# A new order table for the same operations of a gated linear attention followed by a spatial gating unit

## Chip, cores and metric

The kernel runs on one core of a Trainium2 chip. The metric is the device time of one execution in microseconds (us), smaller is better. In the text PE is TensorE (its weight loads are shown apart, as PEld), DVE is VectorE, ACT is ScalarE, POOL is GpSimd and SP is SyncE, from whose queue the DMAs are issued.

## What is computed

Two layers. The first is linear attention with a decaying state, for 4 batches, 8 heads, 768 steps and a head size of 48; the second is a gated unit that mixes over the sequence:

```python
for t in range(S):                                   # S = 768, D = 48
    state = alpha[:, :, t, :, None] * state + einsum('bhd,bhe->bhde', k[:, :, t], v[:, :, t])
    y[:, :, t] = einsum('bhd,bhde->bhe', q[:, :, t], state)
x = y.transpose(0, 2, 1, 3).reshape(B, S, H * D)      # 4 x 768 x 384
h = maximum(x @ w_in, 0.0)                            # 384 -> 1024
u, v = h[..., :512], h[..., 512:]
v_n = (v - mean(v)) / sqrt(var(v) + 1e-06)            # over the last axis
v_s = einsum('ts,bsd->btd', w_spatial, v_n) + b_spatial[None, :, None]
out = (u * v_s) @ w_out                               # 512 -> 384
```

Inputs and output are float32; the kernel works in bfloat16 with float32 sums in PSUM.

## The kernel before

The 768 steps of a batch are cut into 6 chunks of 128, so there are 24 chunks, numbered 0 to 23 over the four batches 0 to 3. The recurrence is solved chunk by chunk with matmuls. Chunks 0 to 3 and 6 to 9 are taken four at a time, chunks 4 and 5 as a pair, the others singly.

The program does not issue instructions as it goes through its loops. It first makes a list of 944 operations (`op(key, engines, emit, deps, take, ...)`), each with the engines that may run it, the operations that it needs, and the PSUM banks that it takes. Then `replay` reads a table, `PLAN`, and issues the operations in the table's order, on the engine that the table names:

```python
for word in plan.split():
    word, *junk = word.split(":")
    word, *banks = word.split("@")
    op, eng = ops[int(word[1:])], LETTERS[word[0]]
    ...
    op.emit(eng)
```

A word `P103@6,4,5,7:512#7:424#7` means: operation 103 on PE, with banks 6, 4, 5 and 7, and before it two matmuls of 512 and 424 columns on a constant tile (`junk`) into bank 7, whose result nobody reads. Each engine runs its own words in the table's order and waits at the head of its queue when an input is not there; what stands behind a waiting instruction on that engine waits too. SP's words are the DMA issues.

The operations, by the names that this text uses (the number behind a name is the chunk or the pair of chunks, or batch and tile, or batch, column block and half):

- `ac`, `kc`, `qc`, `vc`: loads of alpha, k, q and v. With `.4` four chunks at a time, 768 KB each. `w_in`, `w_sp`, `w_out` are loads of weights, followed by casts to bfloat16 (`cast`). `w_sp` is also transposed on PE (`wt`) and evicted (`we`).
- `pr`: products of neighbouring alphas. `ln`: logarithm of alpha (ACT). `half`, `cum`, `cums`: running sums as matmuls. `einv`, `eexp`: exponentials of minus and plus these sums (ACT; `binv` is the tile of the first).
- `kt`, `qt`: k and q times these factors (`kt` on POOL or DVE, `qt` on DVE). `vb`, `vbs`: cast of v. `tr`, `trk`: transposes of `kt` and `qt` on PE, evicted by `ev`, `evs` into `kqT`. `causal`: the POOL selects that make a mask; `one` makes another.
- `upd`: the chunk's addition to the state (PE); `z`, `S`, `sb`: sum, decay and cast of the state. `sc`: scores (PE); `m`, `ms`: scores times mask (DVE, into `ptm`). `pm` spreads v over partitions, evicted by `vp`. `y`, `ya`: the chunk's output (PE); `xe` evicts it into `xT`.
- Second layer: `v`, `u`: the two halves of `x @ w_in`; `ve`, `ue`: their relu and eviction; `bn`: mean and variance of a tile (DVE); `rs`: the inverse root (ACT); `nm`: `shift`, minus mean times root (DVE); `vn`: normalisation, on ACT (line 1091, uses `shift`) or on DVE (line 1095, uses mean and root). `s`: the spatial matmul, first part over tiles 0 to 3, second part over tiles 4 and 5; `se`: adds the bias (DVE); `g`: times u (POOL or DVE); `o`: the matmul with `w_out`; `oe`: its eviction; `st`: the store. The last tile of the last batch is done in two halves of 192 columns, `o.3.5.0` and `o.3.5.1`.

The matmuls `v`, `u`, `s` and `o` use the whole array of 128 x 128; `tr`, `trk`, `wt`, `sc`, `y`, `ya` and `pm` use parts of it. `vn` reads

```python
if e == "ACT":
    nc.scalar.activation(out=vn[n2][:, x, :], in_=v_sb[n2][:, x, :], func=AF.Identity,
                         bias=shift[n2][:, x:x + 1], scale=rstd[n2][:, x:x + 1])
    return
nc.vector.tensor_scalar(out=vn[n2][:, x, :], in0=v_sb[n2][:, x, :], scalar1=mvs[n2][:, x, 0:1],
                        scalar2=rstd[n2][:, x:x + 1], op0=ALU.subtract, op1=ALU.mult)
```

and `nm` is issued for every tile, whichever engine normalises it. After the last operation of the table ten memsets of one column run on POOL.

Of the kernel before, what the change touches and what calls it, by code (L numbers as in the profile page):

```python
# [51 lines left out]
S278 S399 S389 D39 A206 S29 S387 A165 D166 D208 D168 A286 A294 D35 S388 S400 S401 S390 P210@1 P40@4,6 A288 A211 D42
D41 D212 D209 G297 G300 G306 P217@3 P290@1 P219@6 P221@4 A149 A150 A167 A220 D222 A213 D214 D298 P229@2 P237@6 P225@4
A295 D215 D307 A216 A289 D301 A291 A218 P233@5 A292 A296 P238 D239 P230 D231 P226 P43@3,0 P223@6 A44 A45 G27 G28 D304
D227 P234 D235 G303 A224 P46@1,3 P49@0,2 A47 A51 G236 G228 G299 G240 G232 D50 D48 P309@4,7 D310 P312@5,6 P315@0,1
P318@2,3 D316 D313 D311 D314 P249@4 P250 D251 A302 A317 A319 P341@2,7 P335@6,5 D343 A308 A320 A305 P245@1 P246
P321@7,3,4,0 D336 D337 S506 S548 D322 D324 P253@6 P333@7,5 P254 P241@3 P242 S494 D247 D255 A403 A391 A334 A340 P392@6
A323 P348@5,1 A393 D342 A394 S402 P344@2 P338@7 A345 G33 G32 G30 G325 G326 G31 S495 S507 D243 G396 D327 G328 D349 S560
S497 S496 D397 D350 S508 S509 P404@3 A405 A406 G407 P260@4 P257@5 S611 S549 S563 S550 S562 S561 A339 A395 A261 D408
D330 P362@2 P346@3,6 G398 G244 A363 D347 A353 A258 P354@7,1 P410@0,4 D356 D355 A411 P359@3 P413@1 G329 G331 D412  # L60
P351@5 P357@7 G256 G332 A510 G248 G409 P416@4,0 D414 G415 A352 P421@6,2 D418 D364 D417 A358 P369@1 D422 D423 A552 A498
A370 P374@0 A360 A375 P380@7 P499@1 A500 A502 P376@4 P511@0 A514 D361 D371 P419@6 P424@2 A420 A425 A512 A501 A513 A381
P263@3 P426@2 A365 D377 P372@6 A373 D427 D382 P438@4 P436@2 A437 A439 A264 D428 D516 G252 D366 P378@7 P429@6 A430
P440@4 D441 D431 A564 A383 A379 P442@3 A443 G503 G515 G505 P521@6 P272@0 G517 P529@4 P269@2 P266@3 S623 A432 D522
P565@6 D504 D368 P518@1,7 D433 P553@5 D384 D385 D386 S551 D530 D267 A270 A367 A434 A435 P452@2 S613 S614 S612 S624
P453 D454 A554 A555 D558 P444@3 P445 D446 D519 P456@2 P457 D458 D273 G455 S730 S625 G571 A520 A566 A567 A556 G557 S718
G569 A615 G531 A532 D570 P448@3 P449 P468@2 P469 D450 G459 A559 D470 P533@0,5 P524@3,1 G447 S626 S772 S719 G523
P572@7,4 D525 D534 D535 A574 S733 S721 P472@2 P473 P460@0 P461 P575@4 D526 D474 P616@5 A573 A568 A627 D576 D462 S732
S784 S731 S774 S786 S720 P527@1 P536@2 S775 S773 S835 S847 A617 A537 A618 A528 P579@4,6 P588@7,3 D580 G451 G622 G577
G620 S785 P464@0 D581 D621 D590 P584@4 P628@2 D585 D589 P465 A629 A630 A619 D632 D466 A734 G578 P541@6 P538@1 A542  # L70
P482@5 A539 A483 A722 G463 G631 G586 P476@4 G475 G471 G467 P735@2 P634@1,6 D543 P582@5 P591@0 D635 P637@1 P723@7 A636
A583 D477 D638 P640@4,6 D642 D592 A726 A736 A724 A738 A725 P645@5,3 P593@1 D646 D641 D647 G633 G587 P488@6 A489 D540
G639 P604@0 A776 A594 A737 A605 P596@5 P485@4 P777@1 D595 P643@3 P648@6 A544 P479@0 A644 G729 D545 A778 P491@3 A486
P598@4 G741 A547 A597 G727 D606 D480 A649 A607 P602@0 P650@5 P653@6 A492 A780 D740 D546 D599 P745@3 D651 D608 A609
A779 A603 A654 D746 D610 P660@4 D652 A788 D782 D655 P664@5 D728 D783 P662@3 A665 A663 P668@2 P672@0 P600@6 A601 A656
D657 A658 D661 D659 P789@5 A790 A791 G739 P753@3 D754 G781 G755 P680@1 P666@7 P676@6 A839 A747 A667 P673 P677 P681
P669 D674 D678 A851 A792 G679 G793 D682 P799@0 G683 D800 D670 P742@3,4 P692@1 P693 P696@2 D744 P840@4 A743 A841 D794
D694 P757@5,3 P796@0,7 D759 P748@1,6 D758 P697 D801 D749 D750 P688@3 S836 S837 S848 S849 A842 A798 A797 A843 D845
P852@5 A853 A854 D698 S268 S487 S787 S850 S274 S838 G675 G671 P684@7 D856 G844 P685 P706@0 P689 D690 G695 G855 P751@4
P760@2 D686 D761 A707 A752 P803@5,0 P858@6,1 D804 P812@3,4 A859 A860 A756 G802 G691 P703@7 G795 D814 D805 A704 P765@2  # L80
P762@6 A766 P808@1 D809 G699 G687 P700@0 A846 A701 P869@7,4 P864@1,5 D813 S705 S490 S702 G857 P806@2 P815@3 A807 A763
A816 G810 A811 P715@0 D767 D865 D866 P861@1 P820@6 P817@5 P709@3 P824@2 D862 D871 D870 G863 P872@7 A818 D764 P867@5
D873 P828@4 A868 D819 A829 D830 P822@5 A823 A768 A831 D769 D821 P712@7 P874@4 A875 D713 P877@5 P886@6 A887 D832 P884@4
D878 D770 P890@7 P826@6 P888@5 A771 D885 A833 D834 A825 A889 D876 D879 A880 P912@4 P896@2 P900@5 S484 P904@1 D827 D716
P892@0 S478 S708 S493 D881 D882 A883 P893 D894 P905 D906 G895 S717 P897 P901 P916@0 P913 P908@1 P917 P909 D898 G899
D907 D902 A710 S714 S265 A891 S481 S711 D903 P926@5 A927 P923@2 S271 S262 A924 D910 S259 P920@1 P921 G911 D914 D918
D915 S928 S925 P929@2 A930 S931 D919 D922 P941@0 D942 P938@1 A939 S943 S940 P935@5 P932@1 A933 D936 S937 S934
"""

PAIRS = (2,)
QUADS = (0,3)
PLAIN = (0, 2)

SPLIT = ()
SMALL = ()
# [33 lines left out]
def kernel(  # L131
# [295 lines left out]
    def pair(j):  # L427
# [22 lines left out]

        if j not in PLAIN:
            op(("pr", j, 1), "POOL DVE",
# [776 lines left out]
    idle = consts.tile([128, 1], FP32, name="idle")  # L1229
    nc.vector.memset(junk, 0.5)  # L1230
    replay(ops, held, warm, PLAN)
    for _ in range(10):
        nc.gpsimd.memset(idle, 0.0)


# [28 lines left out]
```

## Time and profile before

| | |
|---|---|
| median of 3 runs | 139.98 us (139.69 to 140.05) |
| the profiled execution | 139.9 us, of which 138.1 us from its first to its last instruction |
| granted TensorE clock | 0.998 |
| busy: PE, DVE, ACT, POOL | 129.9, 121.2, 108.8, 87.8 us |
| DMA | 28.66 MB, mean 207 GB/s |

A group row of the profile reads: line, engine, operation, output and inputs, shapes, count, then busy time and mean duration in ns, then the idle time before these instructions and what ended it. A timeline row reads: start in us, duration in us, engine, line, operation, output and inputs, count, and in brackets the idle time ahead of it and what ended that. A line can be that of a helper: 177 and 179 are copies, 183 and 185 relus, 188 products, 1004 the whole-array matmuls of the second layer.

### The profile page before, as it was taken

The page shows a single profiled execution, that of the slowest core. Times are in us where ns is not written, and L with a number is a line of the kernel's source. Part 1 is how long each engine was busy: PE and PEld are TensorE (multiplying, and loading weights), DVE is VectorE, ACT ScalarE, POOL GpSimd, SP SyncE. Part 2 cuts the span into 40 slices and gives each one's busy share as a digit, 9 for nine tenths or more (in the row PEclk, how much of TensorE's full clock was granted, in tenths as well). Part 3 has the DMA queues.
Part 4 walks back from the last instruction along what each step waited for, and adds up shares of the span by engine and source line. Part 5 has one row for each costly group of instructions (what it writes and reads, how often), then busy time and mean ns, then how long its engine had stood idle before and what let it go on. Part 6 is the DMA issues. An engine that isn't in the chain of part 4 may idle for free.

```text
span 138.1 us, 5300 instructions
## 1 busy us (share of the span) xinstructions
PE 129.9 (94%) x2110; PEld 79.6 (58%) x2124; DVE 121.2 (88%) x295; ACT 108.8 (79%) x258; POOL 87.8 (64%) x148
## 2 busy tenths in 40 slices
PE   6798999999999999999999999999999999999990
PEld 3255555665466556656667675655676665565550
DVE  6059999999899999999899999998999999897950
ACT  3483999999999599999959999969979793874221
POOL 7576799979369899950099999420499932002620
PEclk9999999999999999999999999999999999999999
DMA  3999999599989897798999899899910046007554
GB/s 90 372 370 381 347 343 360 136 376 388 339 186 278 162 211 140 141 210 176 206 209 210 169 203 202 168 207 264 209 29 5 0 169 241 0 0 268 190 196 148
DMA packets 76521, 28.66 MB, mean 207 GB/s; under 512 B 63056, under 2 KB 74960, under 8 KB 76496
## 3 DMA queue, kind: packets, MB, share of 16 engines
q1 hardware_dynamic: 76464, 28.32, 77.9%
q8 instruction: 16, 0.26, 0.8%
q14 instruction: 9, 0.07, 0.2%
q0 software_dynamic: 32, 0.00, 0.0%
HBM read 23.60 MB, written 4.72 MB: 205 GB/s over the span
## 4 chain that ended last, share of the span: by engine, by line
PE 56%; ACT 16%; DVE 13%; DMA 5%; issue 4%; POOL 3%; SPq 0%; POOLq 0%; ACTq 0%
PE bank L1004 37%; DMA vc<-in_v_dram 5%; ACT vn L1091 4%; DVE stats L1066 3%; PE bank L943 2%; ACT v_sb L183 2%; PE bank L959 2%; PE bank L415 2%; PE bank L987 2%; DVE uT L185 2%; ACT uT L183 1%; PE bank L835 1%; DVE ptm L842 1%; ACT kqT L177 1%; PE bank L853 1%
## 5 line engine op out<-in xcount | busy, mean ns | idle before, releaser
L188 POOL TENSOR_TENSOR gT<-vs,uT 128x384 bf16<-128x384 f32 x27 | 24.5, 922 | 21.7 <-DVE vs L1151 21.3
L1004 PE MATMUL bank<-w_spT,vn 128*128 128x384 bf16 x192 | 35.0, 327 | 0.5 <-ACT vn L1091 0.3
L1004 PEld LDWEIGHTS <-vn 128*128 128x128 bf16 x192 | 17.6, 98 | 13.2 <-ACT vn L1091 1.7
L188 POOL TENSOR_TENSOR kt<-kc,binv 128x384 bf16<-128x384 f32 x21 | 19.5, 935 | 3.4 <-ACT uT L183 2.2
L1004 PE MATMUL bank<-xT,w_in 128*128 128x384 bf16 x96 | 19.1, 326 | 0.1
L948 DVE TENSOR_TENSOR ptm<-bank,mask 128x512 bf16<-128x512 f32 x28 | 17.9, 681 | 0.5 <-PE bank L943 0.3
L1004 PE MATMUL bank<-w_out_sb,gT 128*128 128x384 bf16 (+1 forms) x100 | 18.3, 320 | 0.0
L1004 PE MATMUL bank<-w_in,xT 128*128 128x512 bf16 x58 | 17.3, 380 | 1.0 <-issue 0.3
L177 ACT COPY kqT<-bank 128x512 bf16<-128x512 bf16 (+1 forms) x20 | 15.5, 814 | 3.4 <-PE bank L770 2.4
L1151 DVE TENSOR_TENSOR vs<-bank,bsp_bc 128x384 f32<-128x384 f32 x31 | 16.2, 550 | 1.9 <-PE bank L1004 1.7
L1066 DVE BATCH_NORM_STATS2 stats<-v_sb 128x6 f32<-128x512 bf16 x24 | 16.4, 683 | 0.6 <-ACT v_sb L183 0.4
L1004 PEld LDWEIGHTS <-w_in 128*128 128x128 bf16 x96 | 8.9, 97 | 7.0 <-issue 1.0
L188 DVE TENSOR_TENSOR qt<-qc,bank 128x384 bf16<-128x384 f32 x24 | 12.8, 543 | 0.1
L183 ACT ACTIVATE v_sb<-bank 128x512 bf16<-128x512 f32 x20 | 11.9, 603 | 1.0 <-PE bank L1004 0.9
L1004 PEld LDWEIGHTS <-gT 128*128 128x128 bf16 x100 | 9.1, 98 | 5.8 <-POOL vb L179 0.2
L1091 ACT ACTIVATE vn<-v_sb,shift,rstd 128x512 bf16<-128x512 bf16 x13 | 10.0, 809 | 2.1 <-DVE shift L1083 2.0
L183 ACT ACTIVATE uT<-bank 128x384 bf16<-128x384 f32 x24 | 11.2, 492 | 0.4 <-DVE shift L1083 0.4
L177 ACT CAST xT<-bank 128x384 bf16<-128x384 f32 x21 | 9.9, 487 | 2.0 <-PE bank L415 1.6
L842 DVE TENSOR_TENSOR ptm<-bank,mask 128x512 bf16<-128x512 f32 x16 | 10.2, 682 | 0.2 <-PE bank L835 0.2
L1004 PEld LDWEIGHTS <-xT 128*128 128x128 bf16 x72 | 6.4, 98 | 6.2 <-issue 0.3
L392 DVE TENSOR_TENSOR zs<-bank,state 128x384 f32<-128x384 f32 x16 | 8.8, 552 | 0.6 <-ACT sbd L177 0.3
L241 PE MATMUL bank<-junk 128*128 128x512 f32 (+3 forms) x16 | 8.0, 629 | 1.1 <-DVE quarters_of L312 1.0
(159 smaller groups left out, 264.7 us busy)
## 6 DMA issues: line engine op xcount, KB each, us to landing
ac<-in_alpha_dram SPq DMA_DIRECT2D x14, 192.0 KB, 4.4
qc<-in_q_dram SPq DMA_DIRECT2D x14, 192.0 KB, 4.3
kc<-in_k_dram SPq DMA_DIRECT2D x14, 192.0 KB, 3.9
vc<-in_v_dram SPq DMA_DIRECT2D x14, 192.0 KB, 4.7
raw_w<-in_moe_w_spatial_dram SPq DMA_DIRECT2D x3, 768.0 KB, 6.7
out_dram<-raw_w SPq DMA_DIRECT2D x11, 192.0 KB, 2.1
out_dram<-o_sb SPq DMA_DIRECT2D x9, 192.0 KB, 2.0
ac<-in_alpha_dram SPq DMA_DIRECT2D x2, 768.0 KB, 6.7
```

Of the source, the lines that this page charges most:

```text
L177: nc.scalar.copy(out=out, in_=in_)
L183: nc.scalar.activation(out=out, in_=in_, func=AF.Relu)
L185: ENG[eng].tensor_scalar_max(out=out, in0=in_, scalar1=0.0)
L188: ENG[eng].tensor_tensor(out=out, in0=in0, in1=in1, op=ALU.mult)
L241: nc.tensor.matmul(out=banks[n][:, 0:cols].rearrange("p (a b) -> p a b", a=4), lhsT=junk, rhs=junk[:, None, 0:cols // 4].to_broadcast([128 ...
L392: lambda _: nc.vector.tensor_tensor(out=zs[i % 3], in0=tp(), in1=state[(i - 1) % 3], op=ALU.add),
L842: nc.vector.tensor_tensor(out=ptm[n2][:, ci, s], in0=banks[sl.bank].rearrange("p (hp t) -> p hp t", hp=HP), in1=mask[:, 3][:, None, :].to_ ...
L948: nc.vector.tensor_tensor(out=ptm[n2][:, ci, s], in0=banks[sl_p[s].bank].rearrange("p (hp t) -> p hp t", hp=HP), in1=mask[:, 2][:, None, : ...
L1004: nc.tensor.matmul(out=ps, lhsT=lhsT, rhs=rhs, start=first and n == 0, stop=last and n == len(pairs) - 1)
L1066: nc.vector.bn_stats(out=stats[tt % 2], in_=v_sb[n2][:, tt, :])
L1091: nc.scalar.activation(out=vn[n2][:, x, :], in_=v_sb[n2][:, x, :], func=AF.Identity, bias=shift[n2][:, x:x + 1], scale=rstd[n2][:, x:x + 1])
L1151: nc.vector.tensor_tensor(out=vs[d], in0=banks[sl.bank][:, 0:TH], in1=bsp_bc[:, th, :], op=ALU.add)
```

## The change

The operations, the functions and all shapes stay. The table is replaced by another one for the same 944 operations, which was searched with the durations that the trace shows for normalisation on ScalarE and for its shifts, and the number of memsets at the end becomes a constant, 16 instead of 10:

```diff
 PLAN = """
-D4 D2 D1 G6 G9 D0 D3 S56 A60 S59 A61 D90 D84 G11 G5 G8 P66@0:512#0:512#0:512#0 P62@1 P63 P70@2 P71 P74@3 A64 A65 P75
...
+D2 D0 D4 D1 G9 G11 G5 G6 D3 S56 S57 S59 S58 A60 S12 S169 S170 A61 S275 S171 D8 P62@0:512#0:512#0:512#0 P66@1 P67 P63
...
 """
...
+IDLE = 16
...
-    for _ in range(10):
+    for _ in range(IDLE):
         nc.gpsimd.memset(idle, 0.0)
```

Which engine runs what, where the two tables differ (number of operations before -> after):

| operation | ACT | DVE | POOL |
|---|---|---|---|
| `vn` | 13 -> 6 | 11 -> 18 | |
| `ue` | 24 -> 27 | 8 -> 5 | |
| `xe` | 21 -> 23 | 3 -> 1 | |
| `vp` | 6 -> 8 | 2 -> 0 | |
| `oe` | 17 -> 18 | 8 -> 7 | |
| `sb` | 6 -> 2 | 0 -> 1 | 10 -> 13 |
| `vbs` | 2 -> 5 | 1 -> 1 | 11 -> 8 |
| casts of weights | 1 -> 4 | | 15 -> 12 |
| `S` | | 5 -> 6 | 15 -> 14 |
| `ev`, `evs` | 20 -> 20 | 14 -> 14 | |
| `kt`, `g` | | 8 -> 6 | 34 -> 36 |
| quarter masks (`triq`) | | 0 -> 1 | 1 -> 0 |

Of the first four `vn` of batch 0, three were on ACT (0, 1, 2) and now one is (2). In batch 2 three were on DVE (0, 3, 5) and now all six are. In batch 3 the last two, 4 and 5, were on DVE and ACT and are now both on DVE.

Parts of the two orders, by names. The first loads on SP:

```
before  ac.0.4 vc.0.4 kc.0.4 qc.0.4 w_in.1 ac.2 kc.2 ac.3.4 qc.2 w_in.0 vc.2 w_sp.0 w_sp.1 kc.3.4 qc.3.4 w_sp.2 vc.3.4
after   ac.0.4 kc.0.4 vc.0.4 qc.0.4 w_in.1 ac.2 kc.2 ac.3.4 qc.2 w_in.0 vc.2 w_sp.0 w_sp.1 qc.3.4 kc.3.4 w_sp.2 vc.3.4
```

POOL and DVE in the opening:

```
POOL before  ident maskq b_sp tri triq vb.1.0 one vb.0.0 causal kt.0.0 cast cast S.1 sb.1 S.2 cast kt.2.1 kt.2.0 pr.3.1 pr.3.2 sb.2 pr.3.3 cast(w_in.0) cast(w_in.0)
POOL after   maskq b_sp tri ident kt.0.1 causal kt.1.1 vb.1.0 cast S.1 cast S.2 sb.0 sb.2 sb.1 kt.2.0 kt.2.1 pr.3.1 pr.3.2 pr.3.3 cast(w_in.0) cast(w_in.0) cast(w_in.0)
DVE before   vb.1.1 vb.0.1 kt.1.0 kt.1.1 kt.0.1 be.1 qt.1.0 qt.0.1 qt.1.1 S.0 qt.0.0 z.1 ev ev ev ev z.2 ms ms ms ms ms ms vp.2 z.3 qt.2.0 qt.2.1
DVE after    triq kt.0.0 kt.1.0 vb.1.1 vb.0.0 ev be.0 qt.0.1 qt.0.0 qt.1.0 S.0 qt.1.1 z.1 ev ev ev z.2 ms ms ms ms z.3 ms ms ms qt.2.1 qt.2.0
```

PE, from `v.0.0` to the end of the weights' transposes; a bar marks a change between whole-array work and work on parts of it:

```
before  v.0.0 | tr.k.2 y.2 sc.3 | v.0.1 | tr.q.2 | v.0.2 | y.3 sc sc | u v.0.3 u cum.4.1 upd.2 cum u u | ya.2 y.4 y.5 wt.0 wt.1 | v.0.4 cum v.0.5 | wt.2 | u cum.4.0 u u s s s s s s s | wt.3 | u s | wt.4 wt.5 tr.k.3 tr.q.3 tr.k.4 tr.q.4 |
after   v.0.0 v.0.2 | tr.k.2 y.1 tr.q.2 | v.0.1 | y.3 sc sc | v.0.3 cum.4.0 u u upd.2 u u | ya.2 y.4 | cum.4.1 | wt.1 wt.0 | v.0.4 | y.5 | cum | wt.2 | v.0.5 cum u u u s s u s s s | wt.3 | s s | wt.4 tr.k.3 | s | wt.5 tr.q.3 tr.q.4 tr.k.4 |
```

From there on the visits to parts of the array follow each other in much the same way in both. The end of PE's order:

```
before  v.3.4 v.3.5 u u u u u, five first parts of s, s.3.0.0.1 ... o.3.1 o.3.0 s.3.3.1.0 s.3.3.1.1 o.3.2 o.3.5.1 o.3.5.0 o.3.4 o.3.3
after   v.3.5 v.3.4 u u u s.3.2.1.0 o.2.3 s.3.1.0.0 u s.3.2.0.0 s.3.0.0.0 s.3.1.0.1 ... s.3.3.1.0 o.3.2 o.3.0 s.3.3.1.1 o.3.1 o.3.3 o.3.5.0 o.3.4 o.3.5.1
```

90 lines of the change are left out of this document (45 added, 45 removed).

## The prediction

> **What bounds the kernel now.** I read the profile's page first, then the busy time by stage, the groups of instructions, and last the timeline at the few places where TensorE waits.
>
> ```profile
> span 138.1 us, 5300 instructions
> ...
> PE 129.9 (94%) x2110; PEld 79.6 (58%) x2124; DVE 121.2 (88%) x295; ACT 108.8 (79%) x258; POOL 87.8 (64%) x148
> ...
> PE 56%; ACT 16%; DVE 13%; DMA 5%; issue 4%; POOL 3%; SPq 0%; POOLq 0%; ACTq 0%
> ```
>
> PE is busy for 129.9 of 138.1 us, and the chain of waits runs through it for 56%. The stages show where the rest is:
>
> ```profile
> 25.00:41.45 16.45, 15.90 (x302) 9.65 (x300) 15.77 (x43) 16.18 (x41) 11.94 (x16) 1.00 0.96 293
> 41.45:78.00 36.55, 36.24 (x647) 23.06 (x647) 35.22 (x77) 32.23 (x81) 27.60 (x41) 1.00 0.95 191
> 78.00:93.00 15.00, 14.81 (x239) 9.24 (x240) 14.71 (x33) 13.65 (x38) 10.82 (x15) 1.00 1.00 197
> ...
> 117.00:134.60 17.60, 17.42 (x107) 9.82 (x104) 14.53 (x37) 8.90 (x23) 3.85 (x13) 1.00 0.35 127
> ```
>
> The first figure after the stage is its length, then come PE, PEld, DVE, ACT and POOL. From 41.45 to 78 PE idles for 0.31 us in 36.55, from 78 to 93 for 0.19. In the middle of this kernel there is almost no wait to take away. What a new order can win lies before 41 us and after 117 us; what it can lose is anywhere. In 78 to 93 DVE has 0.29 us left as well, so there the two engines bind together.
>
> **The engines that change.** Counted over both tables, seven of the 24 normalisations (`vn`) go from ACT to DVE, and eight evictions of 384 columns (three `ue`, two `xe`, two `vp`, one `oe`) go from DVE to ACT.
>
> ```profile
> L1091 ACT ACTIVATE vn<-v_sb,shift,rstd 128x512 bf16<-128x512 bf16 x13 | 10.0, 809 | 2.1 <-DVE shift L1083 2.0
> ...
> L183 ACT ACTIVATE uT<-bank 128x384 bf16<-128x384 f32 x24 | 11.2, 492 | 0.4 <-DVE shift L1083 0.4
> ...
> L1095 DVE TENSOR_SCALAR vn<-v_sb,mvs,rstd 128x512 bf16<-128x512 bf16 x11 | 5.1, 469 | 0.0
> ...
> L185 DVE TENSOR_SCALAR uT<-bank 128x384 bf16<-128x384 f32 x8 | 4.3, 543 | 0.0
> ```
>
> ACT loses 7 x 0.81 = 5.7 us and gains 8 x 0.49 = 3.9. DVE gains 7 x 0.47 = 3.3 and loses 8 x 0.54 = 4.3. The other moves are three operations to DVE and three from it, and on ACT casts against casts; I take them as even. So both engines get about a microsecond less work, and PE gets exactly the same matmuls. `shift` is still made for every tile, also where DVE normalises and does not read it. As PE is the bound, these sums give nothing by themselves; the order does.
>
> **The opening: -0.9 (from -1.2 to 0).** The change loads `kc` second and `vc` third.
>
> ```profile
> 1.23 6.22 DMA vc<-in_v_dram
> ```
>
> ```profile
> 7.54 0.49 ACT L739 ACTIVATE binv<-bank 128x384 bf16<-128x384 f32 x1 [0.57 <-PE bank L716]
> ...
> 9.62 1.98 POOL L353 TENSOR_SCALAR_AFFINE_SELECT mask<-mask 64x128 bf16<-64x128 bf16 x4
> 9.72 1.73 DVE L188 TENSOR_TENSOR kt<-kc,binv 128x384 bf16<-128x384 f32 x3 [1.16 <-ACT binv L739]
> ...
> 11.69 0.91 POOL L188 TENSOR_TENSOR kt<-kc,binv 128x384 bf16<-128x384 f32 x1
> ...
> 11.84 1.47 DVE L188 TENSOR_TENSOR qt<-qc,bank 128x384 bf16<-128x384 f32 x3
> ...
> 14.94 1.41 DVE L179 COPY kqT<-bank 128x512 bf16<-128x512 bf16 x4
> ...
> 16.73 1.28 DVE L842 TENSOR_TENSOR ptm<-bank,mask 128x512 bf16<-128x512 f32 x2
> ...
> 20.16 2.09 POOL L188 TENSOR_TENSOR ac<-ac 128x384 f32<-128x384 f32 x2
> ...
> 20.57 0.55 DVE L179 CAST vb<-bank 128x384 bf16<-128x384 f32 x1
> ...
> 22.81 0.29 PEld L534 LDWEIGHTS <-qt 64*128 64x128 bf16 x16 [0.42 <-DVE qt L188]
> ...
> 23.60 1.16 POOL L179 CAST w_in<-raw_w 128x512 bf16<-128x512 f32 x2
> ...
> 24.98 0.28 PEld L1004 LDWEIGHTS <-w_in 128*128 128x128 bf16 x3
> ```
>
> The second large load landed at 1.23 + 6.22 = 7.45; the first product with the third began at 9.72 (the row blames `binv`, whose first tile ended at 8.03, so it was the load). With `kc` second, `kt` can start behind `binv` at about 8.0, and `tr.k.0` runs long before 12. But `qc` stays fourth, and DVE's `qt` cannot start before about 11.8. From there DVE's queue sets the stage: four `qt`, `S.0`, `z.1`, then copies of `kqT` before the first mask product at 16.73. The change leaves three copies instead of four in front of it (1.41 / 4 = 0.35). `upd.0` came behind the `kt` of 11.69, at 12.60; POOL's new queue from 8.0 is `kt`, `causal`, `kt` and a cast of `vb`: 8.0 + 0.9 + 2.0 + 0.9 + 0.6 = 12.4 with a POOL cast at 1.16 / 2, so 0.2 are won. The cast of `vb` at 20.57 goes to ACT; a DVE operation of this width starts every 1.47 / 3 = 0.49, the figure for it. Together 0.35 + 0.2 + 0.49 = 1.0 at `tr.q.2`, where PE waited 0.42 for `qt`. I take 0.9, since the order of the mask products changes with it. The far end is 0, for `w_in.0` may set the end of this stage: its casts and the first `u` at 24.98 follow each other closely, and POOL's new queue has all three casts behind the three `pr` products. From 20.16 on these are 3 x 1.04 + 3 x 0.58 = 4.9, or 25.0 if POOL comes no sooner; the first `u`, now behind `v.0.3` and `cum.4.0`, is wanted at 24.98 + 0.6 + 0.3 - 0.9 = 25.0. So the cover is just enough.
>
> **Visits to small tiles: +1.0 (from +0.6 to +1.3).** PE work comes in groups that use the whole array and groups on parts of it (`wt`, `tr`, `sc`, `y`). Each change between the two costs:
>
> ```profile
> 31.42 0.48 PEld L1004 LDWEIGHTS <-xT 128*128 128x128 bf16 x3
> 32.32 0.23 PEld L1016 LDWEIGHTS <-w_row 64*128 64x128 bf16 x12 [0.42 <-issue]
> ```
>
> ```profile
> 32.60 0.28 PEld L1004 LDWEIGHTS <-w_in 128*128 128x128 bf16 x3
> ...
> 118.07 1.12 PEld L1004 LDWEIGHTS <-xT 128*128 128x128 bf16 x6
> ...
> 119.31 0.10 PEld L1004 LDWEIGHTS <-w_in 128*128 128x128 bf16 x1
> ```
>
> `v.0.5`, `wt.2` and the step to the next `u` take 32.60 - 31.42 = 1.18 us. Two `v` in a row take 119.31 - 118.07 = 1.24, so one takes 0.62, and the twelve loads of `wt.2` are busy for 0.23. That leaves 0.33 us for going there and back. Before, `ya.2 y.4 y.5 wt.0 wt.1` is one visit, and `wt.4` to `tr.q.4` one; after, the same work is three visits and two. Three more at 0.33 make 1.0. The Trainium skill, "TensorEngine Tiling (Array Packing)", Key Properties, says that changing the tiling mode drains the engine; this rule speaks against the change, and the gap of 0.42 with nothing awaited agrees with it. The skill gives no price for it there, so the sum stays as it is. In the opening one visit falls away (`tr.q.2` joins `tr.k.2`) and one is added (`bb.1` stands between), both under DVE's cover.
>
> **Waits that go: -0.5 and -0.6 (each from -0.8 to 0).**
>
> ```profile
> 35.18 3.07 PEld L1004 LDWEIGHTS <-vn 128*128 128x128 bf16 x20 [0.61 <-ACT vn L1091]
> ```
>
> ```profile
> 125.67 3.20 PEld L1004 LDWEIGHTS <-vn 128*128 128x128 bf16 x21 [0.47 <-ACT vn L1091]
> ...
> 130.49 0.09 PEld L1131 LDWEIGHTS <-ones_row 1*128 1x128 bf16 x1 [0.32 <-issue]
> ```
>
> At 35.18 PE waits 0.61 for the third of three `vn` in a row on ACT. After, one of the first four is on ACT and three on DVE, and the extra visits stand where PE waited for `xT`. PE idles 0.55 in 25 to 41.45; I take 0.5 of it. What is late next there is `kt` of the second batch, behind `kc.3.4`, which is now loaded after `qc.3.4`, and the last casts of `w_sp`; by the new POOL queue PE reaches them about when they are ready. At 125.67 PE waits 0.47 for the last `vn`. The DVE queue ahead of it loses two `ue` and one `oe` (3 x 0.49) and gets one more `vn` (0.4), and the last `vn` costs 0.4 on DVE instead of 0.81: together 1.5 us. PE has some 0.5 less work to cover it with (a `u` and a first part of `s` less, an `o` more). That wait goes, and of the 0.32 at 130.49 a part.
>
> **The end: -0.2 (from -0.4 to 0).** The last output tile to be computed is now a half one.
>
> ```profile
> out_dram<-o_sb SPq DMA_DIRECT2D x9, 192.0 KB, 2.0
> ...
> out_dram<-raw_w SPq DMA_DIRECT2D x2, 96.0 KB, 1.7
> ```
>
> The store is 0.3 shorter, but a whole tile's store is issued just ahead of it on SP. The six more memsets on POOL run behind its last product; POOL has 3.85 us of work in the last 17.6, so they cost nothing unless POOL ends last.
>
> **New waits: +0.7 (from 0 to +2.1).** Where operations change engines, they meet others than before. The trace shows one such meeting:
>
> ```profile
> 90.10 1.11 DVE L1095 TENSOR_SCALAR vn<-v_sb,mvs,rstd 128x512 bf16<-128x512 bf16 x1
> 90.14 0.91 POOL L188 TENSOR_TENSOR kt<-kc,binv 128x384 bf16<-128x384 f32 x1 [2.24 <-ACT uT L183]
> ```
>
> The mean of the eleven `vn` on DVE is 469 ns, 5.16 us in all; without this one it is (5.16 - 1.11) / 10 = 0.41. It took 0.70 more, and ended behind POOL's product. Seven more `vn` can meet POOL so; three hits are 2.1, one is 0.7, and DVE is not last everywhere. I take one.
>
> The sum is -0.9 + 1.0 - 0.5 - 0.6 - 0.2 + 0.7 = -0.5 us: a span of 137.6, and 139.4 us against the profiled execution's 139.9, which is 0.1 below the median of 139.98.
>
> **The rivals.** (a) DVE and POOL collide in the third batch, and it is slower. All six `vn` of that batch are on DVE after the change (three before), in the stage where DVE has 0.29 us left and POOL is busy for 10.82 of 15. Three hits of 0.70 there are 2.1 us on the engine that binds together with PE; from the second one on they exceed what DVE gains. With the other terms unchanged (-1.2 without the new waits) and the small waits of the middle doubled by the delay: -1.2 + 2.1 + 0.2 = +1.1, so 141.0 us. For it speaks the row at 90.10, in just that batch; against it, that ten of eleven were undisturbed. The Trainium skill, "SBUF — State Buffer", Who interferes with whom, says that DVE in a two-port mode and GpSimd exclude each other for whole instructions; that is this rival, and the trace agrees with 1.11 against 0.41. (b) The opening gives little, because the loads and the casts of `w_in` set its end: -0.9 becomes -0.4, the sum is 0, and the time 139.9. (c) No new waits come, and the rest holds: -0.5 - 0.7 = -1.2, so 138.7. (d) That the change does not do what it says: `vn` on ACT was only once the last wait of a stage before 41 us and once after 117, so the corrected durations may matter at these two places alone; that ends within (b).
>
> **How the numbers follow.** A measurement of this kernel can tell about 0.3%, that is 0.42 us, from no change. Forecast 0.40, (a) 0.31, (b) with (d) 0.19, (c) 0.10. The forecast's own range is 138.9 to 139.9, of which about 0.7 lies below 139.56; with (c) that makes faster 0.28 + 0.10 + 0.02 of (b) = 0.40; the same 0.12 + 0.16 = 0.28; slower 0.32, (a) and the end of (b). The range 138.6 to 141.3 leaves out 0.2: half of (c), the end of (a) and a new wait of a kind not seen here.
>
> **What would show it.** Right: `kt` on DVE near 8.4, first mask product near 16.1, `tr.q.2` near 21.9, no wait of PEld for `vn` over 0.3, three more PEld gaps "issue" of 0.3 to 0.4 between 26 and 41 us. Wrong: `vn` on DVE with a mean over 0.55, a wait of DVE or ACT behind PE in 78 to 93, or PE idle for over 0.6 between 41 and 117.

## The result and the profile after

The kernel after takes 138.53 us (median of 18 runs, 138.11 to 141.15), the kernel before, measured beside it, 140.05 (18 runs, 139.49 to 141.31). The one execution of 141.15 counts as slow and is left out of the ratio. The ratio is 0.9892, with a 95% interval from 0.9868 to 0.9915: faster by 1.1%, or 1.5 us. The forecast was 139.4, with a range from 138.6 to 141.3; the measured time lies 0.07 below this range.

The profiled execution of the kernel after took 139.64 us, 1.1 more than its median, so I show a second one of the same kernel as well, which took 138.20. Its page, the lines that answer to those shown of before:

```profile
span 136.4 us, 5312 instructions
...
PE 130.0 (95%) x2122; PEld 79.0 (58%) x2122; DVE 120.0 (88%) x300; ACT 107.6 (79%) x261; POOL 86.7 (64%) x146
...
PE 86%; DMA 5%; issue 2%; ACT 2%; POOL 2%; SPq 0%; DVE 0%; POOLq 0%
```

PE has the same work (129.9 before, 130.0 now), but the chain that ended last now runs through PE for 86% of the span, where it was 56% (it is 60% in the execution of 139.64, where 19% is DMA). The busy time by stage in this execution, with the columns as in the prediction and the stages cut at about the same work:

```profile
24.50:40.77 16.27, 16.22 (x308) 9.46 (x300) 15.59 (x43) 15.82 (x40) 12.34 (x20) 1.00 0.95 288
40.77:76.95 36.18, 36.18 (x653) 22.92 (x645) 34.99 (x76) 33.26 (x82) 26.74 (x38) 1.00 0.96 196
76.95:91.80 14.85, 14.85 (x244) 9.26 (x242) 14.61 (x36) 13.80 (x38) 9.97 (x14) 1.00 0.97 190
...
115.60:133.00 17.40, 17.28 (x122) 10.06 (x109) 13.14 (x35) 8.31 (x22) 5.28 (x20) 1.00 0.19 70
```

PE idles for 0.05 us in the first of these stages (0.55 before), for none in the second and third (0.31 and 0.19 before) and for 0.12 in the last (0.18 before). In this execution nothing came in place of the waits that went. The first stage is shorter by only 0.18 us all the same (16.27 against 16.45), since PE's busy time in it grew from 15.90 to 16.22.

The profiled execution of 139.64 lost most of its time in one place. These are rows of its timeline, of ACT and of PE:

```profile
57.41 0.52 ACT L888 ACTIVATE la<-ac 128x384 bf16<-128x384 f32 x1 [1.09 <-DMA ac<-in_alpha_dram]
...
58.85 0.41 PE L960 MATMUL bank<-ptm,vb 128*32 128x128 bf16 x16 [1.03 <-ACT uT L184]
```

ACT stands for 1.09 us at the logarithm of chunk 15, whose load of alpha was issued at 51.6 and landed at 57.3; the `ue` behind it is late, and PE idles 1.03 us. In the execution of 138.20 the same load was issued at 49.3 and landed at 54.2, so most of the lateness is already there at the issue.

Where the time went can be read by asking when PE starts an operation before which it has done the same set of work in both kernels, taken at the operation's first weight load. In us:

| after the same work, PE starts | before | after (138.20) | difference | in this stretch |
|---|---|---|---|---|
| `y.3` | 23.90 | 23.43 | -0.48 | -0.48 |
| `s.0.2.1.0` | 41.45 | 40.86 | -0.59 | -0.11 |
| `y.12` | 75.43 | 74.53 | -0.90 | -0.31 |
| `o.3.1` / `s.3.3.1.0` | 128.93 | 127.56 | -1.38 | -0.48 |
| `o.3.5.1` / `o.3.3` | 132.23 | 130.60 | -1.63 | -0.25 |
| end of the span | 138.1 | 136.4 | -1.7 | -0.07 |

By its first matmul `o.3.1` starts at 129.09 instead of 128.93 and the difference there is -1.53, so the split between the fourth and the fifth stretch is only good to some 0.15 us.

### The profile page after: what moved, and what is told of

It is laid out like the page before. It is cut to its first block, busy times and chain, and to the rows that moved or that the text cites. A ratio compares the mean times of both kernels' runs of the same rounds, so it can differ in the third digit from the quotient of the medians.

```text
span 137.9 us, 5298 instructions
## 1 busy us (share of the span) xinstructions
PE 130.1 (94%) x2108; PEld 79.4 (58%) x2122; DVE 120.2 (87%) x300; ACT 107.7 (78%) x261; POOL 86.6 (63%) x146
## 4 chain that ended last, share of the span: by engine, by line
PE 60%; DMA 19%; POOL 8%; issue 3%; SPq 3%; ACT 3%; DVE 0%; POOLq 0%; ACTq 0%
PE bank L1005 43%; DMA raw_w<-in_moe_w_spatial_dram 6%; DMA kc<-in_k_dram 5%; DMA raw_w<-in_moe_w_out_dram 4%; DMA ac<-in_alpha_dram 4%; PE bank L960 3%; SPq L883 3%; PE bank L944 2%; PE bank L988 2%; PE bank L416 2%; POOL w_row L180 2%; POOL kt L189 2%; PE bank L932 1%; PE bank L898 1%; POOL state L189 1%
## 5 line engine op out<-in xcount | busy, mean ns | idle before, releaser
L1005 PE MATMUL bank<-w_spT,vn 128*128 128x384 bf16 x192 | 35.6, 327 | 0.0
L189 POOL TENSOR_TENSOR gT<-vs,uT 128x384 bf16<-128x384 f32 x28 | 25.7, 933 | 14.1 <-DVE vs L1152 14.1
L189 POOL TENSOR_TENSOR kt<-kc,binv 128x384 bf16<-128x384 f32 x22 | 20.2, 928 | 22.3 <-ACT binv L908 15.2
L178 ACT COPY kqT<-bank 128x512 bf16<-128x512 bf16 (+1 forms) x20 | 15.0, 793 | 3.1 <-PE bank L988 1.9
L184 ACT ACTIVATE uT<-bank 128x384 bf16<-128x384 f32 x27 | 12.4, 494 | 0.7 <-PE bank L1005 0.6
L178 ACT CAST xT<-bank 128x384 bf16<-128x384 f32 x23 | 10.4, 482 | 1.1 <-PE bank L416 0.8
L242 PE MATMUL bank<-junk 128*128 128x512 f32 (+3 forms) x14 | 8.8, 763 | 1.0 <-DVE junk L1231 1.0
L178 ACT COPY raw_w<-bank 128x384 f32<-128x384 f32 x8 | 3.8, 479 | 7.3 <-PE bank L1005 7.2
```

What stands on the lines that cost most here:

```text
L178: nc.scalar.copy(out=out, in_=in_)
L184: nc.scalar.activation(out=out, in_=in_, func=AF.Relu)
L189: ENG[eng].tensor_tensor(out=out, in0=in0, in1=in1, op=ALU.mult)
L242: nc.tensor.matmul(out=banks[n][:, 0:cols].rearrange("p (a b) -> p a b", a=4), lhsT=junk, rhs=junk[:, None, 0:cols // 4].to_broadcast([128 ...
L1005: nc.tensor.matmul(out=ps, lhsT=lhsT, rhs=rhs, start=first and n == 0, stop=last and n == len(pairs) - 1)
```

## The experiments

Each run is compared with the kernel before, measured beside it on the same chip. The median of before was 139.87 us beside the first four runs below, 139.84 beside the next four, 139.77 beside the four after them and 139.66 beside the last three. All of these kernels end with 16 memsets, except the first joined table, which has 10.

**The kernel after again.**

> The changed kernel again, for a second profiled execution. The profiled execution of after took 139.64 us, 1.1 above its median, and in it PE idles 1.03 us at 57.8, behind ACT, which waited 1.09 us for a load of alpha. Theory L (that wait is a slow load of this one execution): the new profile has a span near 136.5, without that wait, and the span is about 1.6 below before's. Rival K (the wait belongs to the new order): the wait of ACT for alpha near 57 us is there again with 0.5 us or more, and the faster executions must have gained elsewhere.

138.97 us (12 runs), ratio 0.9928 (0.9904 to 0.9952). Its executions lie between 138.2 and 139.6. In its profile, of 139.62 us, alpha was in time, but `w_sp.1` landed at 31.5 instead of 29.65 and POOL waited 1.76 for it; PE had by then lost 0.69 against the execution of 138.20 at `y.3`, mostly by a stall that is taken up further below. So the losses of the slower executions are not always in the same place.

**Half of one table, half of the other.** Three tables were joined from both:

```diff
 first run:   PLAN = words 0 to 299 of after,  then the rest in the order of before (10 memsets)
 second run:  PLAN = words 0 to 299 of before, then the rest in the order of after
 third run:   PLAN = words 0 to 819 of before, then the rest in the order of after
```

> The new order up to the first spatial matmuls of batch 0 (about 44 us, 300 of 944 words), the old order behind it, ten memsets at the end. By the prediction's sum the opening, the visits and the wait for vn near 35 us give -0.9 + 1.0 - 0.5 = -0.4: 0.997 of before. By the two traces, where the same work is reached 0.45 us earlier at 41 to 47 us: 0.997. Rival (the whole gain comes from the opening, since what starts earlier ends earlier): 0.989.

> The other way round: the old order for the first 300 words, the new one behind it, 16 memsets. By the prediction's sum the waits in the tail, the last store and the new waits give -0.6 - 0.2 + 0.7 = -0.1: 0.999. If no new waits come: -0.8, 0.994. If parts add and the opening is worth 0.4 of the measured 1.5, this one is worth 1.1: 0.992.

> The old order for the first 820 words (about 111 us), the new order behind it, 16 memsets: the tail alone. By the prediction's sum -0.6 - 0.2 = -0.8: 0.994. If the middle of the new order carries part of the gain, this is nearer to 1 than the kernel with the whole rest is.

At the seam two operations got another bank than in their own table (in the third run one), where theirs was still held.

They took 143.33, 145.69 and 142.27 us, ratios 1.0247 (1.0210 to 1.0284), 1.0435 (1.0395 to 1.0474) and 1.0197 (1.0149 to 1.0246): each slower than both whole tables, and none of the three expectations held. The first shows what it was made for up to its seam (`tr.q.3` is 0.36 us earlier than before; in the kernel after it is 0.50 earlier), and then PE waits 2.8 us there in two places. The waits of PE of the first, and two rows of PE's timeline and the row of granted clock of the third:

```profile
PE bank L1005 <- DVE zs L393: 2.8, 2, 1.9
```

```profile
116.75 0.81 PE L1005 MATMUL bank<-w_in,xT 128*128 128x512 bf16 x2 [2.75 <-DVE ptm L949]
...
119.22 1.49 PE L1005 MATMUL bank<-w_in,xT 128*128 128x512 bf16 x3
...
PEclk9999999999999999999999999999999995999998
```

A table fixes the PSUM bank of every operation as well as the order. At a seam, the second half takes a bank that the first half's order has not yet freed, and PE waits up to 2.75 us until DVE has read it. After that wait PE also ran for one slice of 3.6 us at a granted clock of 5 tenths: the three matmuls at 119.22 took 1.49 us, where three of their form take 0.82 (as at 30.00 in a fence below). In the second run PE waits 1.15 us for a bank, then 0.92 and 1.17 for results of ACT, and its clock fell too. These runs could not price the parts; they show that a part of a table cannot be cut out and keep its worth, and in the first and the third that the banks are a reason.

**The late load taken out of the way.**

```diff
-... ue.1.1.0 lns.15 o.0.2 cums.12 ... oe.3 ebc.12 ...
+... ue.1.1.0 o.0.2 cums.12 ... ebc.12 lns.15 rs.1.0 ...
```

> The kernel after with one operation moved: ScalarE's log of alpha for chunk 15 (tile la, which waits for the load into ac) goes 26 places back in the table, from ahead of ve.1.2 to behind ebc.12; its one user, the running sum of chunk 15, still comes 30 places later. Theory (in some executions that load lands only at 57.3 us, 5.7 us after its issue, ScalarE stood 1.09 us for it and TensorE 1.03 us behind ScalarE, and this is what separates the slower executions of the kernel after, 139.1 to 139.6, from its faster ones, 138.2 to 138.4): the slower group goes, median 138.3 (138.0 to 138.6), a ratio of 0.988 to before. Rival 1 (loads land late at several places, w_sp among them, and this is one of them): the median moves by under 0.3 from the kernel after's, 138.5 to 139.0, and the two groups stay. Rival 2 (the moved log now holds ScalarE's queue at the new place or delays the running sum): 139.0 to 139.6.

138.98 us, ratio 0.9935 (0.9908 to 0.9963), from 138.47 to 139.79: rival 1. In its profile the 1.03 us at 58 are gone, but the median did not move. The load of alpha cost that one execution its microsecond; it isn't alone what makes the kernel's executions differ.

**The engines of `vn` without the order, and the order without them.**

```diff
 order of after:   -18 vn on DVE, 6 on ACT    +11 on DVE, 13 on ACT, each as in before
 order of before:  -11 vn on DVE, 13 on ACT   +18 on DVE, 6 on ACT, each as in after
```

> The kernel after, in its own order, with the engine of each of the 24 subtractions vn as in the kernel before (13 on ScalarE, 11 on VectorE, where the kernel after has 6 and 18). Theory of the prediction (the waits of TensorE's weight load for vn, 1.7 us in four places before, go because vn takes 0.40 us on VectorE and 0.81 on ScalarE): 0.5 to 1.1 us slower than the kernel after, 139.2 to 139.8, with waits of PEld behind ACT vn of 0.3 us or more back in its profile. Rival (the order of the operations around them carries the gain, and the engines do not matter): within 0.3 us of the kernel after, 138.4 to 139.0, no such wait over 0.2. Second rival (the new order leaves ScalarE less room, and the 0.4 us per subtraction all come to light): 1.5 us slower or more, over 140.3.

> The kernel before, in its own order, with the engine of each vn as in the kernel after (18 on VectorE). Theory of the prediction: the four waits behind ACT vn (1.7 us) go and nothing else changes, 0.5 to 1.1 us faster than before, 138.9 to 139.5. Rival 1 (the engines alone give little, since what frees TensorE there is held by the next operation): within 0.3 of before, 139.6 to 140.2. Rival 2 (in the old order VectorE is the engine that ends last around them, 87% busy, and the moved subtractions push its chain): 0.5 us or more slower than before, over 140.4.

149.41 us, ratio 1.0614 (1.0553 to 1.0674), and 142.94, ratio 1.0213 (1.0181 to 1.0246). The first is the second rival, far stronger than thought, the second is rival 2. The timeline of PE in the first, then in the second, then DVE's in the second:

```profile
99.50 0.24 PE L901 MATMUL bank<-ones_col,la 128*128 128x1 bf16 x4
103.11 4.45 PE L1005 MATMUL bank<-w_spT,vn 128*128 128x384 bf16 x18 [3.36 <-ACT vn L1092]
```

```profile
35.94 3.91 PE L1005 MATMUL bank<-w_spT,vn 128*128 128x384 bf16 x22 [1.04 <-DVE vn L1096]
```

```profile
33.90 0.68 DVE L1067 BATCH_NORM_STATS2 stats<-v_sb 128x6 f32<-128x512 bf16 x1
...
34.71 0.66 DVE L1067 BATCH_NORM_STATS2 stats<-v_sb 128x6 f32<-128x512 bf16 x1
...
35.50 0.70 DVE L1096 TENSOR_SCALAR vn<-v_sb,mvs,rstd 128x512 bf16<-128x512 bf16 x2
```

In the new order the last `vn` of batch 2 to be done, `vn.2.4`, when it is on ACT, stands behind a dozen evictions and exponentials; it is done at 103, and PE waits 3.36 us. The 18 matmuls behind it took 4.45 us, where the kernel after does 18 in 3.09. In the old order `vn` on DVE stands behind the statistics of tiles 4 and 5; the wait of 1.04 us there is one part of the 3.1, and the rest was not followed. So engine and place belong together: the other engines for `vn` cost 3.1 us by themselves, the rest of the change without them 9.6, and both gain 1.5.

**The end alone.**

```diff
-o.3.5.1 oe st  o.3.5.0 oe st  o.3.4 o.3.3 oe oe st st
+o.3.3 oe st  o.3.5.0 oe st  o.3.4 oe st  o.3.5.1 oe st
```

> The kernel before with the end of its table alone in the order of the kernel after: the last four output products in the order o.3.3, o.3.5.0, o.3.4, o.3.5.1 (before: o.3.5.1, o.3.5.0, o.3.4, o.3.3), each followed by its eviction and its store, so that the last store is one of 96 KB and not of 192 KB. Theory of the prediction: 0.2 us faster than before, 139.5 to 139.9. Rival 1: nothing, since o.3.3, which now comes first, waits for the last product g.3.3.1 as long as o.3.5.1 did and the end is the landing of any store: 139.8 to 140.1. Rival 2: slower by 0.3 or more, since the four stores of the end now stand in one line behind each other's evictions: over 140.1.

139.88 us, ratio 1.0000 (0.9976 to 1.0023). In this run `oe` of `o.3.4` is on ACT. The theory's 0.2 would be a ratio of 0.9986, which lies inside this interval; nothing was seen of it, but it is not excluded.

**The visits merged again** (in the kernel after).

```diff
-ya.2 y.4 | cum.4.1 | wt.1 wt.0 | v.0.4 | y.5 | cum.3.0
+ya.2 y.4 wt.1 wt.0 y.5 | cum.4.1 v.0.4 cum.3.0
-s.0.2.0.1 | wt.4 tr.k.3 | s.0.3.0.1 | wt.5
+s.0.2.0.1 s.0.3.0.1 | wt.4 tr.k.3 wt.5
```

> The kernel after with three operations of TensorE moved, so that the three additional visits to small tiles between 29 and 41 us are gone: y.5 stands behind wt.0 and cum.4.1 behind y.5 (ya.2 y.4 wt.1 wt.0 y.5 are one visit instead of three), and s.0.3.0.1 stands ahead of wt.4 (wt.4 to tr.k.4 are one visit instead of two). Theory of the prediction (0.33 us for each visit, 1.0 in all): 1.0 us faster than the kernel after, 137.5 to 138.0 where that one has 138.5 to 139.0. Rival 1, from the starts of TensorE's rows in the trace of after (from 30.36 to 32.86 two v, two cum, y.5 and wt.2 together take 2.50 us, and 1.24 + 0.66 + 0.2 + 0.23 = 2.33 of it is their own work, so that two visits cost 0.17): a visit costs some 0.1 us, and the kernel is 0.1 to 0.4 us faster, 138.2 to 138.8. Rival 2 (y.5 or wt.4 waits at its new place for POOL, which ends the sum for y.5 at about 29.7 us): no gain, or up to 0.5 us slower.

139.13 us, ratio 0.9966 (0.9939 to 0.9994): no gain, rather less than nothing, which is nearest to rival 2. PE's timeline, first the kernel after (138.20), then this one; the rows are `ya.2` and the first `u` behind the merged stretch:

```profile
28.24 0.74 PE L601 MATMUL bank<-ptm,vb 64*32 64x128 bf16 x64
...
30.00 0.82 PE L1005 MATMUL bank<-w_in,xT 128*128 128x512 bf16 x3
30.75 0.35 PE L416 MATMUL bank<-kqT,sbd 128*32 128x128 bf16 x12
31.03 0.34 PE L708 MATMUL bank<-la,lt_quad 128*128 128x384 bf16 x1
...
32.73 1.63 PE L1005 MATMUL bank<-xT,w_in 128*128 128x384 bf16 x9
```

```profile
29.49 0.73 PE L601 MATMUL bank<-ptm,vb 64*32 64x128 bf16 x64
...
34.05 1.72 PE L1005 MATMUL bank<-xT,w_in 128*128 128x384 bf16 x9
```

32.73 - 28.24 = 4.49 us with four visits, 34.05 - 29.49 = 4.56 with two (a bank of `wt` may add a wait of some 0.1 there). The visit of `y.5` alone: it starts 0.75 us behind the start of a `v` that takes 0.62 among others of its kind, and is left after 0.28, with twelve matmuls done. So a visit costs about 0.1, not 0.33. This rests on the one stretch: behind it PE's profile has losses of other kinds (the stall described below, and a wait of PEld of 0.48 for a `vn` at 38.95), so the time of the whole kernel does not price the visits.

**The load order.** First in the kernel before, then undone in the kernel after:

```diff
 before:  -S: ac vc kc qc   D: vb.1.1 vb.0.1 kt.1.0 kt.1.1     +S: ac kc vc qc   D: kt.1.0 kt.1.1 vb.1.1 vb.0.1
 after:   -S: ac kc vc qc                                      +S: ac vc kc qc
```

> The kernel before with one term of the opening alone: kc is loaded second and vc third, and VectorE has kt.1.0 and kt.1.1 ahead of its two casts vb.1.1 and vb.0.1. The order of TensorE stays. Theory of the prediction (kt on VectorE can start at 8.0 to 8.5 instead of 9.72, but qt cannot before the fourth load at 11.8, so the order of the loads alone wins only what VectorE has less to do behind it): kt at about 8.5, and 0 to 0.4 us faster than before, 139.5 to 139.9. Rival (the whole 0.9 of the opening hangs on this load): 139.0 or less. Second rival (vb now lands where VectorE and POOL need it for the first sums, upd.0, and these are later): 0.2 to 0.6 slower, 140.1 to 140.5.

> The kernel after with vc loaded second and kc third, as before; all else stays. The first kt on VectorE then waits for its load until 9.7 us instead of 8.5. Theory (the opening of the kernel after gains 0.45 us at y.3 through this load): 0.4 to 1.0 us slower than the kernel after, 139.0 to 139.8. Rival 1 (VectorE has slack until the fourth load at 11.8 us, and the gain of the opening comes from the operations behind it): within 0.3 of the kernel after. Rival 2 (in the new order kt, its transposes and their evictions all stand ahead of the first sums, so the lost 1.2 us come through whole): 139.7 to 140.3.

142.59 us, ratio 1.0210 (1.0190 to 1.0229), and 140.95, ratio 1.0094 (1.0073 to 1.0116). The first is the second rival and the second is rival 2, each dearer than its price. PE and POOL in the first, DVE in the second:

```profile
14.85 0.86 PE L794 MATMUL bank<-o_sb,kt 32*128 32x96 bf16 x64 [2.74 <-POOL kt L189]
```

```profile
9.83 0.92 POOL L180 CAST o_sb<-vc 128x384 bf16<-128x384 f32 x1 [3.84 <-DMA vc<-in_v_dram]
...
13.88 0.91 POOL L189 TENSOR_TENSOR kt<-kc,binv 128x384 bf16<-128x384 f32 x1
```

```profile
9.70 1.74 DVE L189 TENSOR_TENSOR kt<-kc,binv 128x384 bf16<-128x384 f32 x2 [4.91 <-DMA kc<-in_k_dram]
```

In the old order POOL has a cast of v at its head, which now waits until 9.83 (7.58 before), and with it all that stands behind it: its `kt` starts at 13.88 instead of 11.69, and `upd.0` with it. Undone in the new order, the load shifts DVE's `kt` from 8.4 to 9.7, and PE's `tr.q.0` by 1.8; in its profiled execution the stall described below took another 1.2. The same swap of two loads costs 2.8 us in one order and its undoing about 2 in the other.

**The `vn` of the last batch put back** (in the kernel after).

```diff
-A vn.3.0  D vn.3.1  D vn.3.2  D vn.3.5
+D vn.3.0  A vn.3.1  A vn.3.2  A vn.3.5
```

> The kernel after with the engines of the six vn of the last batch alone as before (vn.3.0 on VectorE; vn.3.1, vn.3.2 and vn.3.5 on ScalarE). Theory of the prediction (the waits of 0.47 at 125.67 us and of 0.32 at 130.49 in the trace of before hang on these): 0.5 to 0.8 us slower than the kernel after. Rival 1, from the run with all 24 put back, which lost 1.1 us between the last u and the second s of this batch: 1.0 to 1.3 us slower. Rival 2 (the gain of the tail lies in the order of the u, s and oe there, not in vn): within 0.3 us of the kernel after.

140.91 us, ratio 1.0089 (1.0069 to 1.0108): some 2 us slower than the kernel after, more than any theory gave. Rows of ACT and of PE:

```profile
117.67 0.81 ACT L1092 ACTIVATE vn<-v_sb,shift,rstd 128x512 bf16<-128x512 bf16 x1 [0.59 <-DVE shift L1084]
118.39 0.47 ACT L184 ACTIVATE uT<-bank 128x384 bf16<-128x384 f32 x1
```

```profile
118.91 0.81 PE L1005 MATMUL bank<-w_in,xT 128*128 128x512 bf16 x3 [1.12 <-ACT uT L184]
...
126.04 4.24 PE L1005 MATMUL bank<-w_spT,vn 128*128 128x384 bf16 x25 [0.96 <-ACT vn L1092]
```

A `vn` on ACT costs twice: PE waits 0.96 for its result, and 1.12 for the bank of a `u` whose eviction stands behind it, because ACT's form must wait for `shift`, which DVE's form doesn't read. 1.12 + 0.96 = 2.08.

**What makes the executions differ.** In four of these runs with the opening of after (both orders of its loads), PE stood still inside one group of matmuls, where no semaphore is waited for. PE's weight loads in the run with the merged visits, 16 loads of `y.3` of which three come ahead of the wait:

```profile
23.44 0.10 PEld L854 LDWEIGHTS <-vb 128*32 128x32 bf16 x3 [0.42 <-DVE kqT L180]
24.70 0.22 PEld L854 LDWEIGHTS <-vb 128*32 128x32 bf16 x13 [1.16 <-issue]
```

Counted from the start, with 0 for the first, it is weight load 352 in all four. Each time PE goes on about 1.4 us after the end of a 16 KB packet of the queue q8 (instruction):

| run | packet starts, ends | PE goes on | later by |
|---|---|---|---|
| the kernel after again, first | 21.76, 22.71 | 24.12 | 1.41 |
| `vn` back | 22.50, 23.46 | 24.92 | 1.46 |
| visits merged | 22.38, 23.32 | 24.70 | 1.38 |
| vc second | 24.24, 25.19 | 26.76 | 1.57 |
| the execution of 138.20 | 20.96, 21.84 | (23.24) | no stall, `y.3` at 23.43 |

(23.24 would be 1.40 behind the packet's end. "`vn` back" is the run with all 24.) In the other profiles of this opening the packet ended between 21.77 and 22.46, and load 352 was held for at most 0.2 us.

The last runs shift this place in the work, by six more weight loads ahead of it:

```diff
-upd.0.pair@6,4,5,7:512#7:424#7
+upd.0.pair@6,4,5,7:512#7:256#7:56#7:56#7:56#7
```

> The kernel after with the two warm-up products ahead of upd.0 cut into five of the same 936 columns in sum, so that TensorE's stream has six more weight loads and six more products ahead of everything behind 12 us, and the block of instructions that TensorE stood for in y.3 (weight load 352) begins six loads earlier in the work, at v.0.1, where TensorE waits for xT until 22.7 us anyway. Theory (this block is fetched by a packet of the queue q8 instruction, which is asked for some 66 loads ahead of its first use and is usable 1.4 us after its end; between asking and use lie 2.4 us in the kernel after, 3.0 in the kernel before, and 3.0 after this shift): no stall with nothing awaited in y.3; the slower executions become rarer, median 138.2 to 138.6, 0.2 to 0.7 below the kernel after in the same call. Rival 1 (the landing of the loads themselves decides, and the fetch is one of their victims among others): within 0.2 of the kernel after. Rival 2 (the next blocks now fall where TensorE has less time, or the five small warm-up products take longer than two): 0.3 or more slower.

> The kernel of the run before this one in the list (the stream shifted by six weight loads) with the log of alpha for chunk 15 moved 26 places back as well, so that neither the fetch at 23 us nor a late load at 57 us should hold the chain. Theory: 138.2 to 138.4, nearly all executions in the faster group, ratio to before 0.987 to 0.989. Rival: 138.5 to 139.1, since the slower executions have a third cause (w_sp, which lands between 29.6 and 31.5 us).

> The kernel after unchanged, on the same chip as the two shifted ones: 138.5 to 139.0, with executions in two groups; if its profiled execution is a slower one, TensorE stands at weight load 352 (y.3), at the first users of w_sp (29 to 33 us) or at the log of alpha (57 us).

They took 139.22 us (ratio 0.9970, 0.9943 to 0.9997), 139.87 (1.0005, 0.9979 to 1.0030) and, for the kernel after, 138.47 (0.9917, 0.9882 to 0.9952). Of the first, the fastest of 12 took 138.95. PE's timeline in it:

```profile
23.57 0.19 PE L535 MATMUL bank<-ident,qt 64*128 64x64 bf16 x1 [0.98 <-issue]
```

The stall has moved in the work and stayed in the stream: it is now ahead of the last matmul of `tr.q.2`, at load 352 again, and ends 1.40 after the packet's end at 22.17; with `lns.15` moved as well, 1.45 after 22.95. So PE waits for its instructions there, and not for data: that part of the theory held. The remedy failed (by its time, rival 2). The packet does not start earlier; it started at 21.21 and 22.00, within the spread of the others with this order of loads (20.90 to 22.50), while PE now needs it some 0.9 us sooner. That fits that even the fastest execution is 0.75 slower than the profiled one of the kernel after. Why the run with `lns.15` moved as well is slower still stays open. The Trainium skill, "Runtime: NRT & Kernel Launch", Instruction fetch mechanics, says that each engine's instructions come in blocks of 16 KiB over a DMA queue of its own, and that crossing a block is mostly hidden; the packets of 16 KB agree, and the stalls, of 0.4 to 1.5 us by PE's rows, show that it was not hidden here. What starts the packet, and whether the loads beside it (DMA at 9 tenths or more from 3.4 to 24 us by the page) hold it up, was not settled.

## Why the prediction was wrong, and where it was right

**The term that failed is "new waits: +0.7".** The prediction took one meeting of DVE and POOL, at 0.70, as a cost of every execution. All 18 `vn` on DVE, in the execution of 138.20, in the kernel after again and in the run with the stream shifted:

```profile
L1096 DVE TENSOR_SCALAR vn<-v_sb,mvs,rstd x18: 383/405/410, 32.1 to 122.2; 128x512 bf16<-128x512 bf16 x18
```

```profile
L1096 DVE TENSOR_SCALAR vn<-v_sb,mvs,rstd x18: 382/406/970, 33.1 to 123.6; 128x512 bf16<-128x512 bf16 x18
```

```profile
L1096 DVE TENSOR_SCALAR vn<-v_sb,mvs,rstd x18: 381/405/1106, 33.1 to 123.7; 128x512 bf16<-128x512 bf16 x18
```

The columns are the shortest, median and longest duration in ns. Not one of 18 was lengthened in the first. In the second, one took 970 ns beside a cast and a `kt` on POOL, and PEld waited 0.6 for it. The Trainium skill, "SBUF — State Buffer", Who interferes with whom, states this exclusion (DVE in a two-port mode and GpSimd block each other for a whole instruction), and the rows agree that it exists. The meeting hangs on another delay. It is the same `vn` each time, `vn.0.4`, near 38 us. Eleven profiles have the opening of after. In six of them PE stood for 0.39 us or more at weight load 352 (the four of the table above and the two shifted ones), and in just these six `vn.0.4` took 0.73 to 1.11 us beside a `kt` on POOL, and PEld waited 0.31 to 0.71 for it. In the five others it took 0.40 to 0.41. So a late opening is paid for a second time there: in the run with the stream shifted PE is 1.01 later than in the execution of 138.20 at `y.3`, and 1.65 later at the `s` that reads this `vn`. In the five profiles whose opening was in time the term was nothing. Without it the sum is rival (c): 138.7, against a median of 138.53; that it comes so near is partly luck, since two other terms missed in opposite ways (below). In the middle, 41 to 75 us, the new order even took 0.31 out, in a stage of which I had said that it had almost no wait to take away: it had 0.31 of idle time, and all of it went. Of the marks for "wrong" two appeared. PE idled for over 0.6 between 41 and 117, but of the profiles of the kernel after only in the one with the late load of alpha. And ACT waits 0.52 for PE at 78.8, which it did not before; that cost nothing, since PE does not idle in this stage.

**The opening was half as large:** 0.48 us at `y.3` instead of 0.9. `kt` on DVE started at 8.43 (8.4 was named), the first mask product at 16.15 (16.1), `tr.q.2` at 22.02 (21.9). These steps are right. But then:

```profile
22.02 0.29 PEld L535 LDWEIGHTS <-qt 64*128 64x128 bf16 x16
22.67 0.33 PEld L1005 LDWEIGHTS <-xT 128*128 128x128 bf16 x3 [0.36 <-ACT xT L178]
23.43 0.23 PEld L854 LDWEIGHTS <-vb 128*32 128x32 bf16 x16 [0.42 <-DVE kqT L180]
```

Of 22.81 - 22.02 = 0.79 won at `tr.q.2`, `v.0.1` gives back a part, since ACT's `xT` is now late, and 0.48 is left at `y.3`. I followed DVE's queue to `tr.q.2` and did not ask what is late next behind it.

**The visits were mis-sized,** +1.0 for about 0.2 to 0.4. I took the step from `v.0.5` over `wt.2` to `u`, 1.18, and subtracted the 0.23 for which the weight loads of `wt.2` are busy. By PE's own rows, `u` starts 0.28 behind the start of `wt.2` (32.32 to 32.60), and a gap of PEld is no gap of PE: the loads run ahead of the matmuls. The gaps that I named as the mark are there in PEld, two of them in the execution of 138.20:

```profile
30.75 0.18 PEld L416 LDWEIGHTS <-sbd 128*32 128x32 bf16 x12 [0.42 <-POOL w_row L180]
...
31.46 0.23 PEld L1017 LDWEIGHTS <-w_row 64*128 64x128 bf16 x12 [0.32 <-POOL le_one L346]
```

But PE idles for 0.05 us in the whole stage. The Trainium skill, "TensorEngine Tiling (Array Packing)", Key Properties, says that a change of mode drains the engine; the trace has room for some 0.1 us of it, and the stretch with two visits merged away was no shorter.

**The waits that go** went: no wait of PEld for `vn` over 0.1 us is left in the executions of 138.20 and 139.64 (1.7 us in four places before). Together the first wait and the visits should have given +0.5 between 24 and 41 us; it was -0.11. The second wait and the last store should have given -0.8; from 75.4 us to the end it was -0.48 - 0.25 - 0.07 = -0.80. The sum is right, though not its parts: the last store alone gave nothing, and the run with the last four `vn` put back shows that they are worth 2 us in this order.

So three terms missed and partly cancelled (opening 0.4 too good, visits 0.6 to 0.8 too bad), and the new waits tipped it. The forecast of a load or a fetch that comes too late was missing altogether: it is there, but only in part of the executions. The median of 138.53 is 0.3 above the fastest profile, 138.20; that these late loads and fetches make up this difference is argued from a few profiles and not shown for the 18 runs.

None of these runs beats the kernel after.

## What to carry to other kernels

When a table or a scheduler moves operations between engines, price engine and order as one: here each alone cost 3 to 10 us and the pair gained 1.5. A collision that comes only when something else is late is a rival with its condition, not a term of the sum; and a gap in PE's weight loads has to be looked for in PE's own rows before it counts. Where a profiled execution lies a microsecond from its median, profile the same kernel again before explaining either.

## What was not expected of the hardware

PE can stall inside a group of matmuls for 0.4 to 1.5 us because its next 16 KB of instructions have not come: in six of eleven profiles with this opening, always at weight load 352, until 1.4 to 1.6 us after the packet's end. The delay then lets a `vn` on DVE meet a `kt` on POOL, and PE pays again.

In three runs the granted clock fell to 0.50 for 3.41 us in the middle of the work. In the 3.41 us ahead of the fall PE had been busy for 0.68 us (the third joined table, after one wait of 2.75 us), 0.69 (the order of after with the old engines of `vn`, in its wait of 3.36 us) and 1.32 (the second joined table, after waits of 1.15, 0.92 and 1.17 us). So short waits close together did it too, while one wait of 2.74 us, at 14.85 in the old order with `kc` second, left the clock at 1.00. What decides was not tested. After the wait of 3.36 us, 18 matmuls took 4.45 us instead of 3.09: a stall can be paid by half again.
